# Two heads scored a batch ahead, their V beside the dense chain, in a two-layer decode kernel

## The chip, the core and the metric

The kernel runs on one core of one Trainium2 chip. The metric is the device time of one execution in microseconds; the median of several runs counts. A core has five engines with instruction queues of their own: TensorE (PE; its weight loads are PEld), VectorE (DVE), ScalarE (ACT), GpSimd (POOL) and SyncE (SP), which here only issues DMAs. TensorE writes to PSUM; the rest of the data lies in SBUF.

## The reference

Eight batches, one token each, pass twice through the same two blocks: attention over a cache, then a small MLP.

```python
def _A_ref(x, k_cache, v_cache, wq, wo):           # x: 8 x 1 x 448
    q = (x @ wq).reshape(8, 1, 16, 256).transpose(0, 2, 1, 3)
    k = jnp.repeat(k_cache, 2, axis=1)             # caches: 8 x 8 heads x 4096 x 256, bf16
    v = jnp.repeat(v_cache, 2, axis=1)
    p = _softmax(jnp.einsum("bhqd,bhkd->bhqk", q, k) * 256 ** -0.5)
    o = jnp.einsum("bhqk,bhkd->bhqd", p, v)
    return o.transpose(0, 2, 1, 3).reshape(8, 1, 4096) @ wo

def _B_ref(x, w1, w2, w3, w4):
    ...            # S = 1: every shifted part of h is zero, so x1 = x
    return x1 + _gelu(_layernorm(x1) @ w3) @ w4

x = x + _A_ref(_layernorm(x), ...)
x = x + _B_ref(_layernorm(x), ...)
x = x + _A_ref(_layernorm(x), ...)                 # the same caches and weights again
x = x + _B_ref(_layernorm(x), ...)
```

The caches are 134 MB each and are needed in both layers; everything else is small.

## The kernel before

**Units, parts and steps.** A unit `(p, b, g)` is one KV head `g` (two query heads) of batch `b` in pass `p` (1 for the first attention, 2 for the second). Its 4096 keys are four parts of 1024 keys, 512 KB of K and 512 KB of V each. The list `units` is the order of work. The main loop walks it, unit `t`, quarter `q`, and calls the pair a step, numbered `4 * t + q`. In a step, `k_part` (L573) multiplies one part of K by the spread query: 16 matmuls into scores. `v_part` (L552) multiplies one part of V by the exponentials of an earlier unit: 16 matmuls into the sum of its head. Between them stands the scoring of the unit before: `max_reduce` (L588, DVE), `max_mms` (L596, PE), `exps` (L606 DVE and L609 ACT), `to_rows` (L622 and L632 PE, L636 ACT) and `sums` (L643 DVE, L644 POOL). V part `s` of unit `t` comes in step `4 * t + s + LAG`, LAG being 6; those of the last unit before a chain come earlier, so that steps 4 and 5 of a chain have none. This is the dictionary `plan`.

**Slots.** All K and V pass through 31 slots of SBUF (512 KB each). `loads` is the list of loads in the order of their use. `pump` issues the next one from SyncE (L462) whenever a slot is free beyond one in reserve. A K part lands raw, is transposed by two DVE instructions into a second slot (`transposes`, L486), which frees the first. The list `by` spreads these transposes evenly over the steps between the borders of the chains. A V part frees its slot when `v_part` is through.

**Kept heads.** Of the eight heads of a batch, the K of six (2 to 7) is kept in its slots after pass 1 and used again in pass 2; the K of the "loose" heads 0 and 1 is read twice. Two parts of the 24 kept ones are parked in PSUM and copied back by ACT (L458). Around a chain, then, 22 of 31 slots hold kept K.

**Order of a batch.** Pass 1 of the kept heads; then the dense chain; then, behind a border called the fence, pass 2 of the kept heads. The dense chain (`mid_steps`, one piece a step) is the output projection (L175), layer norm (L204 to L239), the MLP (L131, L306), layer norm and the second q (L131, L338), all for one batch. Beside it stand units that need nothing of it: loose heads of pass 2 of earlier batches and of pass 1 of later ones.

```python
for b in range(Bn):
    units += [(1, b, g) for g in heads[(len(loose) if b else 0) :]]
    ends[len(units) - 1] = b
    n2 = (0, 2, 2, 2, 2, 2, 1, 3)[b]
    n1 = (4, 2, 2, 2, 1, 1, 2, 0)[b]
    units += [after.pop(0) for _ in range(n2)] + [early.pop(0) for _ in range(n1)]
    fence[len(units)] = b
    units += [(2, b, g) for g in second]
```

So four units (16 steps) stand beside each of the first four chains, three (12 steps) beside the others. `make_blocks` spreads q for a run of up to three heads (`expand`, L154 on PE, L160 on ACT), two steps before the run begins, or, at the fence, as soon as the new q is there. The last units are the two loose heads of pass 2 of the last batch; then comes the last MLP for all batches at once.

Of the kernel before, what the change touches and what calls it, by code (L numbers as in the profile page):

```python
# [17 lines left out]
RESERVE = 1  # L18
KEEP = 6
PARKED = 2  # L20
RUN = 3
LEAD = 1
LAG = 6

# [2 lines left out]
def kernel(  # L27
# [59 lines left out]


    qT1 = consts.tile([128, HJ, Bn], BF16, name="qT1")
    qT2 = consts.tile([128, HJ, 3], BF16, name="qT2")  # L90
    Qblk = [consts.tile([128, RUN, 4, 2, 4, 2], BF16, name=f"Qblk{i}") for i in range(2)]


# [73 lines left out]
    PO = 8 * Bn  # L167
    n_po = (512 - PO) // 4
    OT = consts.tile([128, HJ, 2], BF16, name="OT")

    def wo_mms(y, o, g):

# [81 lines left out]
    def mid_steps(b, spread):  # L254

        xs = X[:, b, :]
        res = {}

        def first():
            nc.vector.tensor_tensor(out=xs, in0=xs, in1=y1[:, b, :], op=ALU.add)
            total(xs)

        between.append(first)
        yield
        norm_rows(xs, res)
# [30 lines left out]

        between.append(gelu)
        yield  # L300
        yield
        yp = room(4)
        for cs in bursts(4, 2, spread):
            for c in cs:
                for m in range(HC):
                    nc.tensor.matmul(  # L306
                        yp[:, c : c + 1],
                        chunk(w4_sb[:, m, :], c),
                        hT[:, m : m + 1],
                        start=(m == 0),  # L310
                        stop=(m == HC - 1),
                    )
# [12 lines left out]
        yield  # L325

        variance(((256.0, 256.0 * EPS),))
        q2 = qT2[:, :, b % 3].rearrange("p (i m) -> p i m", i=2)
        qp = room(HJ).rearrange("p (i m) -> p i m", i=2)
        for ms in bursts(HJ // 2, 3 if spread else 2, True):  # L330
            in_mms(
                qp[:, :, ms[0] : ms[-1] + 1].unsqueeze(3), wq_sb, wq_tl, res["rows"], HJ, ms, True
            )
            if ms[-1] + 1 < HJ // 2:
                yield

        def scaled():
            nc.scalar.mul(q2, qp, nr[:, 0:1])  # L338
            q_done.add(b)

        between.append(scaled)
# [5 lines left out]

    second = heads[G - KEEP // 2 :] + heads[G - KEEP : G - KEEP // 2]
    parked = {(second[-1], 4 - PARKED + i): i for i in range(PARKED)}
    early = [(1, b, g) for b in range(1, Bn) for g in loose]  # L350
    after = [(2, b, g) for b in range(Bn - 1) for g in loose]
    units = []
    ends = {}
    fence = {}
    for b in range(Bn):
        units += [(1, b, g) for g in heads[(len(loose) if b else 0) :]]
        ends[len(units) - 1] = b

        n2 = (0, 2, 2, 2, 2, 2, 1, 3)[b]
        n1 = (4, 2, 2, 2, 1, 1, 2, 0)[b]  # L360
        units += [after.pop(0) for _ in range(n2)] + [early.pop(0) for _ in range(n1)]
        fence[len(units)] = b
        units += [(2, b, g) for g in second]
    units += [(2, Bn - 1, g) for g in loose]
    n_units = len(units)
    assert not early and not after and len(set(units)) == n_units == 2 * Bn * G

    def fresh(u, s):

        return u[0] == 1 or u[2] in loose  # L370


    runs = {}
    run_of = []
    t = 0
    while t < n_units:
        p, b, g = units[t]
# [29 lines left out]


    plan = {}
    for t in range(n_units):  # L410
        for s in range(4):
            i = 4 * t + s + LAG
            if t in ends:
                i = 4 * t + (6, 6, 7, 7)[s]
            elif t + 1 == n_units:
                i = 4 * t + (5, 5, 6, 7)[s]
            plan.setdefault(i, []).append((t, s))
# [4 lines left out]
    for i in range(4 * n_units + 8):  # L422
        while k < by[min(i, 4 * n_units - 1)]:
            loads.append(("k",) + parts[k])
            k += 1
        loads += [("v",) + p for p in plan.get(i, [])]
        t, q = divmod(i + 2, 4)
        if t < n_units and units[t][0] == 2 and (units[t][2], q) in parked:
            loads.append(("p", t, q))
    loads.reverse()  # L430
    free = list(slots)
# [61 lines left out]
            pump()  # L493


    pts, scs, mzs, pos = {}, {}, {}, {}
    dense = []

    def dense_next():
# [6 lines left out]
    def make_blocks(t):  # L506

        if t in runs and t not in ready:
            p, b, g = units[t]
            if p == 1 or b in q_done:  # L510
                x, n = runs[t]
                qT = qT1[:, :, b] if p == 1 else qT2[:, :, b % 3]
                expand(Qblk[x], qT[:, 4 * g : 4 * (g + n)], n, scb[t % 2])
                ready.add(t)

    def head_out(t):

        p, b, g = units[t]
        for h in range(2):
            k = 4 * g + 2 * h  # L520
            o = OT[:, k : k + 2, b % 2] if p == 1 else qT1[:, k : k + 2, b]
            nc.scalar.mul(o, pos[t][:, :, h], rzs[t % 2][:, h : h + 1])  # L522

    def mark(t):


        p, b, g = units[t]
        if p == 1:

            gs = [g]  # L530
            if b and g in loose:
                return
            if b and g - len(loose) in loose:
                gs = [g - len(loose), g]
            for k in gs:
                wo_mms(y1[:, b, :].unsqueeze(2), OT[:, :, b % 2 : b % 2 + 1], k)
        elif b == Bn - 1:
            wo_mms(y2, qT1, g)
        if t in ends:
            dense.append(mid_steps(b, spread[b]))  # L540

    def v_part(t, s):
        if s == 0:
            at = PO + 4 * (t % n_po)
            pos[t] = pyb[:, at : at + 4].rearrange("p (k h) -> p k h", h=2)
            if t == n_po // 2:
                nc.vector.memset(pyb[:, PO : PO + 4 * (n_units - n_po)], 0.0)
        v = v_of.pop((t, s))
        vv = v[:].rearrange("p (c d) -> p c d", d=Dh)
        for c in range(8):  # L550
# [66 lines left out]
    def to_rows(t):  # L617
# [12 lines left out]
        for c in range(4):  # L630
            sel = rows32[:, c].rearrange("p b r -> p (b r)")
            nc.tensor.matmul(pp[:, c], sel, pe[:], start=True, stop=True)  # L632
        pts[t] = work.tile([128, 32, 2], BF16, tag="pt", name="pt")
        for pb in range(4):
            sl = slice(32 * pb, 32 * pb + 32)
            nc.scalar.copy(  # L636
# [4 lines left out]
    def sums(t):  # L641
        zz = mzs[t][:, 256:320].rearrange("p (c h) -> p h c", h=2)
        nc.vector.tensor_reduce(zs, zz, AX.X, ALU.add)  # L643
        nc.gpsimd.tensor_tensor(out=rzs[t % 2], in0=zs, in1=mone, op=ALU.pow)  # L644


    identb = slots[-4][:, 1024:1152]
# [57 lines left out]
    for t in range(n_units + 1):  # L705
        cur = t < n_units
        for q in range(4):
            i = 4 * t + q
            if cur:
# [8 lines left out]
                flush()  # L718
                if not late and not beside[t]:
                    transposes(i)  # L720
                k_part(t, q)
            if q == 0 and t:
                max_mms(t - 1)
                exps(t - 1)
            if cur and late:
                transposes(i)
            if t and q == 1:
                to_rows(t - 1)
                sums(t - 1)
            if q == 2 and not cur:  # L730
# [9 lines left out]
            dense_next()  # L740
            if q > 1:
                make_blocks(t + 1)
            if cur and q == 3:
                max_reduce(t)
    mark(last)
    flush()
# [110 lines left out]
```

## Time and profile before

| | |
|---|---|
| median of 3 runs | 1132.48 us (1129.94 to 1134.14) |
| profiled execution: its own time, its span | 1134.93 us, 1133.2 us |
| read from HBM | 446.77 MB, 394 GB/s over the span |
| PE, DVE, ACT, POOL busy | 61%, 49%, 26%, 9% of the span |
| loads of V and K | 512 and 320, of 512 KB each |
| granted clock of TensorE | 1.000 |

The profile is of one execution. Its page has the busy shares, the span in 40 slices, the DMA queues, the chain of work that ended last, and the costliest groups of instructions. The trace behind it answers for stretches of time, lists who waited for whom, and shows instructions in the order of time, each with the idle time before it and what ended that in brackets. A name such as `SPq L462` is an engine (`q`: its queue) and a line of the kernel before.

### The profile page before, as it was taken

Reading aid. Unit: us, or ns where it says so; the run is one execution under the profiler, and the core shown is the slowest. Engines: PE = TensorE matmul, PEld = TensorE weight load, DVE = VectorE, ACT = ScalarE, POOL = GpSimd, SP = SyncE. Lnnn points to the kernel's source line nnn. Section 1 sums busy time; section 2 is a strip of 40 time slices with the busy share of each in tenths; the row PEclk is TensorE's granted clock in tenths of the full one; section 3 lists DMA queues with packets and bytes.
Section 4 is the critical chain, followed back from the end, with each engine's and each line's share of the span. In section 5 each row is a group of like instructions: output and inputs, shape, how many; then the busy total and the mean of one; then the engine's idle time right before and its main releaser. Section 6 shows DMA issues by size and latency. Waiting matters only on the chain.

```text
span 1133.2 us, 46689 instructions
## 1 busy us (share of the span) xinstructions
PE 689.6 (61%) x20665; PEld 624.5 (55%) x20665; DVE 556.7 (49%) x1305; ACT 293.1 (26%) x1280; POOL 104.2 (9%) x156
## 2 busy tenths in 40 slices
PE   3155665657656576565656666565765666565665
PEld 3144655556555565565655565565655565565665
DVE  5265645446454554545545464545544454546332
ACT  1012123222322223221232214222232214221241
POOL 0000010001000010000000010000100000000011
DMA  9999999999999999999999999999999999999993
GB/s 362 383 418 417 407 399 416 417 405 387 417 417 416 398 392 415 416 417 374 402 417 416 417 375 387 417 417 415 358 416 416 416 384 409 417 416 406 355 417 132
DMA packets 127194, 449.80 MB, mean 397 GB/s; under 512 B 13568, under 2 KB 19600, under 8 KB 126608
## 3 DMA queue, kind: packets, MB, share of 16 engines
q1 hardware_dynamic: 126992, 446.83, 98.9%
q8 instruction: 161, 2.64, 0.8%
q14 instruction: 41, 0.34, 0.1%
HBM read 446.77 MB, written 0.01 MB: 394 GB/s over the span
## 4 chain that ended last, share of the span: by engine, by line
DMA 71%; PE 13%; DVE 5%; issue 5%; ACT 3%; SPq 2%; POOL 0%; POOLq 0%; DVEq 0%; ACTq 0%
DMA slot<-in_A_v_cache_dram 42%; DMA slot<-in_A_k_cache_dram 28%; PE bank L552 3%; DVE slot L486 3%; PE bank L573 3%; PE bank L131 2%; SPq L462 2%; ACT pt L636 2%; PE bank L231 1%; PE bank L632 1%; ACT pe L609 1%; DVE small L606 1%; PE bank L596 0%; PE bank L622 0%; PE bank L139 0%
## 5 line engine op out<-in xcount | busy, mean ns | idle before, releaser
L552 PE MATMUL bank<-pt,slot 128*128 128x2 bf16 x8192 | 302.0, 166 | 361.3 <-DMA slot<-in_A_v_cache_dram 327.3
L552 PEld LDWEIGHTS <-slot 128*128 128x128 bf16 x8192 | 265.6, 105 | 414.7 <-DMA slot<-in_A_v_cache_dram 380.4
L486 DVE STREAM_TRANSPOSE slot<-slot 128x512 f32<-128x512 f32 x640 | 415.9, 688 | 146.7 <-DMA slot<-in_A_k_cache_dram 131.6
L573 PE MATMUL bank<-Qblk,slot 128*128 128x8 bf16 x8192 | 294.9, 168 | 24.2 <-issue 15.4
L573 PEld LDWEIGHTS <-slot 128*128 128x128 bf16 x8192 | 263.7, 104 | 28.7 <-issue 22.5
L644 POOL TENSOR_TENSOR small<-small 128x2 f32<-128x2 f32 x128 | 89.3, 698 | 970.7 <-DVE small L643 970.7
L609 ACT ACTIVATE pe<-bank,small 128x32 bf16<-128x32 f32 x256 | 61.1, 296 | 449.9 <-DVE small L606 449.9
L636 ACT CAST pt<-bank 32x64 bf16<-32x64 f32 x512 | 103.8, 203 | 142.8 <-PE bank L632 138.4
L606 DVE TENSOR_REDUCE small<-bank 128x2 f32<-128x256 f32 x128 | 54.0, 422 | 154.0 <-PE bank L596 154.0
L643 DVE TENSOR_REDUCE small<-bank 128x2 f32<-128x64 f32 x128 | 28.4, 221 | 160.9 <-ACT pt L636 119.6
L588 DVE TENSOR_REDUCE small<-bank 128x2 bf16<-128x64 f32 x128 | 27.2, 213 | 88.1 <-PE bank L573 88.0
L160 ACT CAST Qblk<-bank 32x48 bf16<-32x48 f32 (+2 forms) x200 | 37.4, 187 | 101.1 <-PE bank L154 87.3
L632 PE MATMUL bank<-pe,rows 128*128 128x64 bf16 x512 | 51.0, 241 | 0.0
L596 PE MATMUL bank<-rows,small 128*128 128x128 bf16 x256 | 48.0, 291 | 1.9 <-DVE small L588 1.9
L522 ACT ACTIVATE OT<-bank,small 128x2 bf16<-128x2 f32 x128 | 26.9, 261 | 70.1 <-PE bank L552 68.9
L175 PEld LDWEIGHTS <-wo_sb 128*128 128x128 bf16 x1152 | 35.4, 104 | 6.8 <-issue 6.8
L632 PEld LDWEIGHTS <-rows 128*128 128x128 bf16 x512 | 33.7, 124 | 8.6 <-issue 7.5
L175 PE MATMUL bank<-OT,wo_sb 128*128 128x1 bf16 x1024 | 33.1, 165 | 5.0 <-ACT OT L522 5.0
L131 PEld LDWEIGHTS <-wq_sb 128*128 128x128 bf16 x864 | 29.9, 106 | 8.5 <-DMA wq_sb<-in_A_wq_dram 4.5
L622 PE MATMUL bank<-pe,small 128*128 128x64 bf16 x128 | 27.3, 213 | 7.2 <-ACT pe L609 4.4
L458 ACT COPY slot<-park 128x1024 bf16<-128x1024 bf16 x32 | 30.8, 1015 | 3.1 <-PE bank L552 2.9
L522 ACT ACTIVATE qT<-bank,small 128x2 bf16<-128x2 f32 x128 | 27.0, 265 | 7.8 <-PE bank L552 4.2
(108 smaller groups left out, 321.3 us busy)
## 6 DMA issues: line engine op xcount, KB each, us to landing
slot<-in_A_v_cache_dram SPq DMA_DIRECT2D x512, 512.0 KB, 9.9
slot<-in_A_k_cache_dram SPq DMA_DIRECT2D x320, 512.0 KB, 9.9
wo_sb<-in_A_wo_dram SPq DMA_DIRECT2D x4, 896.0 KB, 9.3
wq_sb<-in_A_wq_dram SPq DMA_DIRECT2D x3, 1024.0 KB, 6.9
w_sb<-in_B_w_dram SPq DMA_DIRECT2D x1, 1568.0 KB
w_sb<-in_B_w_dram SPq DMA_DIRECT2D x3, 448.0 KB, 10.3
wq_tl<-in_A_wq_dram SPq DMA_DIRECT2D x2, 256.0 KB, 10.1
w_tl<-in_B_w_dram SPq DMA_DIRECT2D x2, 112.0 KB, 9.3
```

Of the source, the lines that this page charges most:

```text
L131: nc.tensor.matmul(pv[:, i, j, :], cols(big[:, c, :], m + i * half), rows[:, c, :], start=(i == 0 and j == 0 and c == 0), stop=True, skip_ ...
L175: nc.tensor.matmul(y[:, c, :], chunk(wo_sb[:, k, :], c), o[:, k, :], start=False, stop=True, skip_group_check=True,)
L486: nc.vector.transpose(dst[:, q], src[:, q])
L522: nc.scalar.mul(o, pos[t][:, :, h], rzs[t % 2][:, h : h + 1])
L552: nc.tensor.matmul(pos[t][:, k, :], vv[:, c, 128 * k : 128 * k + 128], pts[t][:, 8 * s + c, :], start=(t == 0 and s == 0 and c == 0 and k ...
L573: nc.tensor.matmul(scs[t][:, 2 * s + c, :, :], ktv[:, db, c, :, x], Qblk[run_of[t][0]][:, run_of[t][1], db, x, :, :], start=(db == 0 and x ...
L596: nc.tensor.matmul(mzs[t][:, 128 * h : 128 * h + 128], pm[:, h : h + 1].to_broadcast([128, 128]), ident, start=True, stop=True,)
L606: nc.vector.tensor_reduce(nm, mx, AX.X, ALU.max, negate=True)
L609: nc.scalar.activation(pe[:].rearrange("p c b h -> p h (c b)")[:, h], scs[t].rearrange("p c b h -> p h (c b)")[:, h], ACT.Exp, bias=nm[:, ...
L632: nc.tensor.matmul(pp[:, c], sel, pe[:], start=True, stop=True)
L636: nc.scalar.copy(pts[t][sl].rearrange("p (k c) h -> p k c h", c=4), pp[sl, :, :, pb, :].rearrange("p c k h -> p k c h"),)
L644: nc.gpsimd.tensor_tensor(out=rzs[t % 2], in0=zs, in1=mone, op=ALU.pow)
```

## The change

Every chain gets two units without K, `GAP`, one ahead of and one behind its one or two whole units (`lone`). In their four steps nothing is transposed for them or scored; V parts and the dense chain go on. Two heads a chain (`ahead`) are scored earlier: most of them are the loose heads of pass 2 of the batch before, which now stand in the middle of that batch's kept heads (third to fifth place behind the fence), and before the first chain two loose heads of pass 1 of batch 1. Their exponentials and reciprocals stay in tiles of their own (`pt_far`, `rz_far`), and their eight V parts are read and multiplied in steps 0, 1 and 4 to 9 of the next chain (`late_v`). The V parts of a whole unit that stands ahead of a `GAP` are due before the fence. The chains keep their 16 and 12 steps. `RUN` goes from 3 to 2, and the second q has two buffers instead of three. In all there are 144 units in place of 128, 16 of them `GAP`.

```diff
-RUN = 3
+RUN = 2
+AHEAD = 2
...
-    early = [(1, b, g) for b in range(1, Bn) for g in loose]
-    after = [(2, b, g) for b in range(Bn - 1) for g in loose]
+    GAP = None
+    ahead = {b: [(2, b - 1, g) for g in loose] for b in range(1, Bn)}
+    ahead[0], ahead[6] = [(1, 1, g) for g in loose], [(2, 5, 0), (1, 7, 0)]
+    lone = {b: [(1, b + 2, g) for g in loose] for b in range(4)}
+    lone.update({4: [(1, 6, 0)], 5: [(1, 6, 1)], 6: [(1, 7, 1)], 7: [(2, 5, 1)]})
...
+    late_v = {}
+    half = KEEP // 2
     for b in range(Bn):
-        units += [(1, b, g) for g in heads[(len(loose) if b else 0) :]]
+        if b:
+            units += [(1, b, g) for g in heads[len(loose) :]]
+        else:
+            units += [(1, b, g) for g in heads[:-half]] + ahead[0] + [(1, b, g) for g in heads[-half:]]
         ends[len(units) - 1] = b
-
-        n2 = (0, 2, 2, 2, 2, 2, 1, 3)[b]
-        n1 = (4, 2, 2, 2, 1, 1, 2, 0)[b]
-        units += [after.pop(0) for _ in range(n2)] + [early.pop(0) for _ in range(n1)]
+        at = 4 * len(units)
+        ps = [(units.index(u), s) for u in ahead[b] for s in range(4)]
+        late_v.update(zip(ps, [at + i for i in (0, 1, 4, 5, 6, 7, 8, 9)]))
+        units += [GAP] + lone[b] + [GAP]
         fence[len(units)] = b
-        units += [(2, b, g) for g in second]
+        units += [(2, b, g) for g in second[:half]] + ahead.get(b + 1, []) + [(2, b, g) for g in second[half:]]
     units += [(2, Bn - 1, g) for g in loose]
...
-    for t in range(n_units):
+    for t in order:
         for s in range(4):
-            i = 4 * t + s + LAG
-            if t in ends:
+            i = late_v.get((t, s), 4 * t + s + LAG)
+            if t in ends or units[t + 1 : t + 2] == [GAP]:
                 i = 4 * t + (6, 6, 7, 7)[s]
...
-        pts[t] = work.tile([128, 32, 2], BF16, tag="pt", name="pt")
+        if (t, 0) in late_v:
+            held.append(t)
+            pts[t] = work.tile([128, 32, 2], BF16, tag="pt_far", name="pt_far", bufs=AHEAD)
+        else:
+            pts[t] = work.tile([128, 32, 2], BF16, tag="pt", name="pt")
...
-        nc.gpsimd.tensor_tensor(out=rzs[t % 2], in0=zs, in1=mone, op=ALU.pow)
+        rz_of[t] = rzs[nth[t] % 2]
+        if (t, 0) in late_v:
+            rz_of[t] = rz_far[:, held.index(t) % AHEAD, :]
+        nc.gpsimd.tensor_tensor(out=rz_of[t], in0=zs, in1=mone, op=ALU.pow)
...
-                k_part(t, q)
-            if q == 0 and t:
+                if units[t]:
+                    k_part(t, q)
+            back = t and units[t - 1]
+            if q == 0 and back:
                 max_mms(t - 1)
                 exps(t - 1)
```

More of the change, by code (lines that the diff above doesn't have):

```diff
@@ L89 @@
     qT1 = consts.tile([128, HJ, Bn], BF16, name="qT1")
-    qT2 = consts.tile([128, HJ, 3], BF16, name="qT2")
+    qT2 = consts.tile([128, HJ, 2], BF16, name="qT2")
     Qblk = [consts.tile([128, RUN, 4, 2, 4, 2], BF16, name=f"Qblk{i}") for i in range(2)]
@@ L169 @@
     OT = consts.tile([128, HJ, 2], BF16, name="OT")
+    rz_far = consts.tile([128, AHEAD, 2], FP32, name="rz_far")
     def wo_mms(y, o, g):
@@ L327, in mid_steps @@
         variance(((256.0, 256.0 * EPS),))
-        q2 = qT2[:, :, b % 3].rearrange("p (i m) -> p i m", i=2)
+        q2 = qT2[:, :, b % 2].rearrange("p (i m) -> p i m", i=2)
         qp = room(HJ).rearrange("p (i m) -> p i m", i=2)
@@ L354 @@
     fence = {}
+    late_v = {}
+    half = KEEP // 2
     for b in range(Bn):
-        units += [(1, b, g) for g in heads[(len(loose) if b else 0) :]]
+        if b:
+            units += [(1, b, g) for g in heads[len(loose) :]]
+        else:
+            units += [(1, b, g) for g in heads[:-half]] + ahead[0] + [(1, b, g) for g in heads[-half:]]
         ends[len(units) - 1] = b
-        n2 = (0, 2, 2, 2, 2, 2, 1, 3)[b]
-        n1 = (4, 2, 2, 2, 1, 1, 2, 0)[b]
-        units += [after.pop(0) for _ in range(n2)] + [early.pop(0) for _ in range(n1)]
+        at = 4 * len(units)
+        ps = [(units.index(u), s) for u in ahead[b] for s in range(4)]
+        late_v.update(zip(ps, [at + i for i in (0, 1, 4, 5, 6, 7, 8, 9)]))
+        units += [GAP] + lone[b] + [GAP]
         fence[len(units)] = b
-        units += [(2, b, g) for g in second]
+        units += [(2, b, g) for g in second[:half]] + ahead.get(b + 1, []) + [(2, b, g) for g in second[half:]]
     units += [(2, Bn - 1, g) for g in loose]
     n_units = len(units)
-    assert not early and not after and len(set(units)) == n_units == 2 * Bn * G
+    order = [t for t in range(n_units) if units[t]]
+    nth = {t: n for n, t in enumerate(order)}
+    assert len({units[t] for t in order}) == len(order) == 2 * Bn * G
     def fresh(u, s):
-        return u[0] == 1 or u[2] in loose
+        return u is not GAP and (u[0] == 1 or u[2] in loose)
     runs = {}
@@ L376 @@
     while t < n_units:
+        if units[t] is GAP:
+            run_of.append(None)
+            t += 1
+            continue
         p, b, g = units[t]
@@ L427 @@
         t, q = divmod(i + 2, 4)
-        if t < n_units and units[t][0] == 2 and (units[t][2], q) in parked:
+        if t < n_units and units[t] and units[t][0] == 2 and (units[t][2], q) in parked:
             loads.append(("p", t, q))
@@ L493, in transposes @@
             pump()
-    pts, scs, mzs, pos = {}, {}, {}, {}
+    pts, scs, mzs, pos, rz_of, held = {}, {}, {}, {}, {}, []
     dense = []
@@ L511, in make_blocks @@
                 x, n = runs[t]
-                qT = qT1[:, :, b] if p == 1 else qT2[:, :, b % 3]
+                qT = qT1[:, :, b] if p == 1 else qT2[:, :, b % 2]
                 expand(Qblk[x], qT[:, 4 * g : 4 * (g + n)], n, scb[t % 2])
@@ L521, in head_out @@
             o = OT[:, k : k + 2, b % 2] if p == 1 else qT1[:, k : k + 2, b]
-            nc.scalar.mul(o, pos[t][:, :, h], rzs[t % 2][:, h : h + 1])
+            nc.scalar.mul(o, pos[t][:, :, h], rz_of[t][:, h : h + 1])
     def mark(t):
+        if units[t] is GAP:
+            return
         p, b, g = units[t]
@@ L543, in v_part @@
         if s == 0:
-            at = PO + 4 * (t % n_po)
+            at = PO + 4 * (nth[t] % n_po)
             pos[t] = pyb[:, at : at + 4].rearrange("p (k h) -> p k h", h=2)
-            if t == n_po // 2:
-                nc.vector.memset(pyb[:, PO : PO + 4 * (n_units - n_po)], 0.0)
+            if nth[t] == n_po // 2:
+                nc.vector.memset(pyb[:, PO : PO + 4 * (len(order) - n_po)], 0.0)
         v = v_of.pop((t, s))
@@ L726 @@
                 transposes(i)
-            if t and q == 1:
+            if back and q == 1:
                 to_rows(t - 1)
@@ L742 @@
                 make_blocks(t + 1)
-            if cur and q == 3:
+            if cur and units[t] and q == 3:
                 max_reduce(t)
```

## The prediction

> **What bounds the kernel now.** I read the page first: busy shares, the chain that ended last, the DMA lines.
>
> ```profile
> DMA  9999999999999999999999999999999999999993
> GB/s 362 383 418 417 407 399 416 417 405 387 417 417 416 398 392 415 416 417 374 402 417 416 417 375 387 417 417 415 358 416 416 416 384 409 417 416 406 355 417 132
> DMA 71%; PE 13%; DVE 5%; issue 5%; ACT 3%; SPq 2%; POOL 0%; POOLq 0%; DVEq 0%; ACTq 0%
> ```
>
> The DMA share hides the dips; the rate below it shows them. Most slices run at 416 to 418 GB/s; about eight times the rate sinks to 358 to 400. The chain is 71% DMA, and nearly every byte is cache that must be read (832 loads of 512 KB), so time can only come out of the dips, the start or the tail. The change leaves start and tail alone.
>
> Next, busy time by stretch. The rows of the first block are stretches around a dense chain (last head of pass 1, chain, first units of pass 2); the row of the second is a stretch between chains. Columns: window, length, busy of PE, PEld, DVE, ACT, POOL, clock, DMA share, GB/s.
>
> ```profile
> 98.00:165.00 67.00, 41.76 (x1239) 38.09 (x1236) 37.18 (x91) 14.60 (x70) 6.13 (x9) 1.00 1.02 405
> 504.00:570.00 66.00, 42.55 (x1266) 39.02 (x1263) 36.03 (x90) 14.70 (x70) 6.13 (x9) 1.00 1.00 392
> 640.00:696.00 56.00, 36.26 (x1104) 33.83 (x1100) 30.09 (x78) 12.91 (x62) 5.43 (x8) 1.00 0.99 381
> 765.00:823.00 58.00, 37.12 (x1118) 34.45 (x1116) 30.00 (x78) 12.90 (x62) 5.43 (x8) 1.00 1.00 387
> 1016.00:1072.00 56.00, 36.73 (x1111) 34.12 (x1108) 28.44 (x75) 12.91 (x62) 5.43 (x8) 1.00 0.99 381
> ```
> ```profile
> 696.00:765.00 69.00, 43.20 (x1307) 38.40 (x1304) 32.79 (x67) 21.32 (x88) 6.28 (x9) 1.00 1.03 416
> ```
>
> Loss of a stretch = length × (417 − rate) / 417. With the three rows not shown (399, 397 and 396 GB/s in 66, 66 and 54 us) that is 1.9, 2.8, 3.2 and 4.0 us for the four chains of 16 steps and 4.8, 4.2, 2.7 and 4.8 for the four of 12 steps: 11.9 + 16.5 = **28.4 us**, all that can be won.
>
> Third, the sixth chain close up: SyncE's issues, then TensorE.
>
> ```profile
> 805.64 0.80 SPq L462 DMA_DIRECT2D slot<-in_A_v_cache_dram  x2
> 812.35 0.33 SPq L462 DMA_DIRECT2D slot<-in_A_k_cache_dram  x1
> ```
> ```profile
> 805.90 0.23 PE L154 MATMUL bank<-qT,rows 128*128 128x12 bf16 x3
> 808.78 0.17 PE L154 MATMUL bank<-qT,rows 128*128 128x12 bf16 x1 [2.65 <-issue]
> 809.84 0.57 PE L573 MATMUL bank<-Qblk,slot 128*128 128x8 bf16 x16 [0.89 <-ACT Qblk L160]
> ```
>
> At the fence no load is issued for over 6 us. The kept K tiles hold their slots until the new q is spread, and V parts already landed hold theirs until their step comes (LAG is 6). By the issue and landing times, loads outstanding fall from 6 to 2; those issued at 812.77 and 813.98 then land 2.56 and 2.41 us after the one before, instead of 1.25. A shallow queue costs bandwidth.
>
> Fourth, who waits inside the chains: the third (16 steps), then the sixth (12 steps).
>
> ```profile
> PE bank L552 <- DMA slot<-in_A_v_cache_dram: 4.9, 3, 2.7
> DVE slot L486 <- DMA slot<-in_A_k_cache_dram: 5.5, 5, 1.9
> ```
> ```profile
> PE bank L154 <- issue: 2.7, 1, 2.7
> PE bank L231 <- DVE small L222: 1.4, 2, 0.9
> ```
>
> The long chains still wait for data now and then. The short ones do not: TensorE is late there, and landed data sits in slots.
>
> **The change, part by part.** *Loads.* None is removed: 512 V and 320 K before and after, 16 parked copies in both. Only order and lifetime change.
>
> *The chain's steps.* Counted from the plan, a long chain before has 16 K parts transposed and scored and 16 V parts multiplied; after, 8 and 22. A short chain has 12 and 12, then 4 and 18. A part is 16 matmuls, 0.43 us on TensorE either way (the starts at 802.70 and 803.12). Scoring a unit (L596, L622, L632) is 0.37 + 0.21 + 0.40 = 0.98 us; two units fewer are scored in either chain and just behind its fence. So TensorE saves 2 × 0.43 + 2 × 0.98 = 2.8 us of a chain. VectorE loses eight parts of two 0.69 us transposes (1.3 us a part, L486) and two units of 0.42 + 0.22 + 0.21: 12 us of a chain. That work stood ahead of the chain's small operations on the same engine (center, scale, gelu).
>
> *Slots.* From step 4 of a short chain to its fence, slots given back are 8 K + 6 V before and 4 K + 10 V after: 14 both times. Steps 4 and 5, which before have no V part at all, have one each. The larger difference is at the fence: before, the last unit's six remaining V parts straddle it; after, the K-less unit has multiplied every V part due, and the eight slots that hold raw K or V belong to loads for later steps. I expect 5 to 7 outstanding where the trace shows 4 to 6, some 9 us of transfers at 1.25 us each, which covers the 4 us of 805.9 to 809.8.
>
> *What it gives back.* Behind the fence the first six steps now have no V part, so one slot comes free a step and not two; another eight V-less steps follow at the two heads scored ahead. A step of a kept unit with its V part takes 1.1 to 1.5 us there once data has landed (TensorE's K parts start at 813.96, 815.21, 816.27 and 817.78), without V some 0.4 less: about one slot a microsecond, against one load per 1.25 us. Balanced, with the queue as reserve. Bounds: nothing, or 0.5 us for each of 14 steps in eight batches, 56 us, if a V-less step lasted 1.75 us. The rows lie near the first end; I put 2 us.
>
> *Smaller parts.* RUN 2 makes 76 spreads of q instead of 50: 26 × 4 casts of 187 ns (L160) = 19 us more on ScalarE, which is 26% busy, and 26 × 0.25 us on TensorE. Each is made two steps ahead, behind L636 and L522 of the unit before; who waits is the next K part, which in the whole trace waited 4.6 us for it in five places. Between chains TensorE is busy 43 of 69 us, so this hides under loads; without that cover it is up to 26 us. Held exponentials and reciprocals go to tiles of their own, the same casts and the same 0.70 us GpSimd power: nothing. No queue is passed by anything new: SyncE issues in the new order, and the parked copies (L458, 1.0 us each) stay behind the same units. The V wait in front of the chain's first addition comes behind two more V loads, 2.5 us, within a stretch that its loads fill anyway: nothing. The two K-only heads before the first chain cost VectorE 1.5 us a step (1.3 + a quarter of 0.85) against 1.25 us of load for eight steps, 2 us, under 19 loads of reserve: nothing.
>
> **The sum.** In the long chains TensorE and VectorE work shrinks while loads still set the pace: I take three quarters of 11.9 us, 9. In the short ones as many slots come free for as much TensorE time, so mainly the hole at the fence closes: a quarter of 16.5, 4. Less 2 behind the fences: 11 us. The profiled execution took 1134.93 us (span 1133.2 and 1.7 around it), which gives 1124; it stands 2.4 us over the median, 1132.48, which gives **1121.5**.
>
> On the shallow queue: with three and four loads outstanding the trace has 2.4 us and more between landings. The Trainium skill ("DMA: Bandwidth & Descriptors", Anatomy of one DMA) puts a fixed 2 us plus bytes at 436 GB/s on a DMA, fitted on another issuing path; by that, as an estimate, a load alone takes 3.2 us and three outstanding keep the rate. The trace disagrees with it.
>
> **Rivals.** *Every hole closes.* If the queue never runs shallow the whole 28.4 us come back: 1104. For it: the eight slots at the fence. Against it: nearly as many slots come free for nearly as much TensorE time in a short chain. (The page's fixed cost would give the same, since five outstanding would then be more than enough.)
>
> *Same holes, other place.* The 14 = 14 slots above speak for it: short chains keep their 16.5, the long ones win some 4 and the fences take 2 back: gain 0 to 5, 1127.5 to 1133. Against it: six V parts stuck at the fence are gone.
>
> *Slower: V-less steps starve the queue.* One slot a step in the 14 V-less steps of a batch. It decides once such a step lasts over 1.25 us by more than the queue covers; at 1.75 us a batch loses 14 × 0.5 = 7 us, some 5 beyond the cover, 40 in eight batches, less the 11 won: 1161. For it: scoring is a round trip over four engines (L588, L596, L606, L609, L632), with no V work between. Against it: those kept units with V run at 1.1 to 1.5 us a step.
>
> *Slower: TensorE's clock.* K-less units leave TensorE waiting for V loads. If the granted clock halved there, 28 parts and some 8 us of chain matmuls would take up to 20 us longer in a chain, half of it beyond the loads: some 80 us, 1200. Against it: in the slice from 40 to 50 us TensorE was busy 1.0 of 10 us and the granted clock stayed 1.00. The Trainium skill ("TensorE: Matmul & The Clock Gate", What's actually happening) says that the clock halves after about 3.4 us idle; that slice speaks against it.
>
> **How the numbers follow.** A measurement of this kernel can tell about 0.5% (5.7 us) from no change. The forecast (gain 6 to 20) has 0.56, every hole closed 0.04, same holes 0.21, V-less starvation 0.16, the clock 0.03: faster 0.60, same 0.21, slower 0.19. The low end of the range is a gain of 20 (1112), the high end takes in the same holes and a mild starvation (1138). The forecast's own range is 1112 to 1127.
>
> **What would show it.** Right: the chain stretches at 400 GB/s or more, no issue hole over 4 us at a fence, outstanding loads never under 3, K parts behind the fence about 1 us apart, the stretches between at 416, clock 1.00. Wrong: dips just behind the fences or at the two heads scored ahead, TensorE waiting there for scores, or short chains still at 381 to 387.

## The result and the profile after

| | before | after |
|---|---|---|
| median of 20 runs each, us | 1133.53 (1129.94 to 1135.78) | 1136.01 (1133.76 to 1139.9) |
| ratio after / before | | 1.0025, 95% interval 1.0015 to 1.0035 |
| profiled execution: own time, span, us | 1134.93, 1133.2 | 1135.04, 1133.0 |

The changed kernel is slower by 0.25%. That is inside the half per cent that the prediction called "same", but the interval excludes no change. The forecast was a gain of 11 us. The two profiled executions differ by 0.1 us only: that of before lies above its median, that of after below its own. So the traces show where time moved, and the 2.5 us between the medians have to come from the timed runs.

The page of after: the rate in the 40 slices, the chain of work that ended last by engine, and the spreads of q (group row; busy and mean ns, then idle before).

```profile
GB/s 361 386 417 418 413 391 415 417 416 399 416 416 417 407 392 413 417 417 400 406 415 417 417 396 358 417 416 417 363 400 417 416 411 372 416 417 417 372 415 77
DMA 66%; PE 16%; DVE 6%; issue 5%; ACT 4%; SPq 2%; POOL 0%; POOLq 0%; DVEq 0%; ACTq 0%
L161 ACT CAST Qblk<-bank 32x32 bf16<-32x32 f32 (+1 forms) x304 | 53.0, 174 | 81.8 <-PE bank L155 78.0
```

The dips of the first four chains are shallower in sum, those of the last four are still there (358, 363, 372, 372). The chain of waits has moved five points away from DMA: three to TensorE, one each to VectorE and ScalarE. The casts of q cost 15.6 us more on ScalarE (37.4 us before).

Busy time by stretch in after: one long chain and the four short ones, a stretch between chains, then the end of the kernel in two parts. Columns: window, length, busy of PE, PEld, DVE, ACT, POOL, clock, DMA share, GB/s.

```profile
109.00:168.00 59.00, 37.17 (x1096) 34.00 (x1092) 27.53 (x72) 11.91 (x58) 4.75 (x7) 1.00 1.02 403
646.00:706.00 60.00, 39.80 (x1187) 36.78 (x1185) 25.22 (x68) 13.77 (x68) 4.75 (x7) 1.00 0.98 379
772.00:832.00 60.00, 39.68 (x1198) 36.93 (x1194) 25.20 (x68) 13.70 (x68) 4.75 (x7) 1.00 0.98 384
899.00:955.00 56.00, 36.93 (x1121) 34.52 (x1119) 23.59 (x65) 12.52 (x62) 4.75 (x7) 1.00 0.99 391
1024.00:1080.00 56.00, 35.93 (x1080) 33.51 (x1078) 19.73 (x59) 14.14 (x63) 4.75 (x7) 1.00 1.00 393
706.00:772.00 66.00, 41.17 (x1232) 37.74 (x1230) 37.34 (x77) 22.18 (x95) 6.99 (x10) 1.00 1.03 416
1080.00:1112.00 32.00, 22.27 (x713) 21.32 (x711) 9.23 (x23) 11.98 (x52) 2.86 (x5) 1.00 0.96 388
1112.00:1133.00 21.00, 11.17 (x327) 10.53 (x327) 5.26 (x25) 2.74 (x12) 4.64 (x5) 1.00 0.01 3
```

By the prediction's formula the long chains lose 7.9 us instead of 11.9 (rates 403, 408, 399 and 402 in 59, 63, 58 and 56 us), the short ones 16.9 instead of 16.5. VectorE is relieved in the short chains (25 of 60 us, 30 of 56 to 58 before); TensorE is not (39.8 of 60, 36.3 of 56 before). Between chains the rate is 416 as before, and the clock is 1.00 everywhere.

The last row is the other half of the story. Before, it reads:

```profile
1116.00:1133.20 17.20, 7.95 (x221) 7.29 (x220) 4.62 (x23) 2.18 (x10) 4.01 (x4) 1.00 0.01 3
```

In after the last load landed at 1111.5 us, 4.5 us earlier than before (1116.1). But the work behind it took 21.5 us instead of 17.1. The stream won 4.5 us and the tail gave back 4.4.

**The sixth chain in after**, as shown of before: SyncE's issues (start, duration to the last of the group, count), TensorE, VectorE, then TensorE's waits from 783 to 822 us (total, times, longest).

```profile
807.96 0.33 SPq L478 DMA_DIRECT2D slot<-in_A_k_cache_dram  x1
808.39 0.38 SPq L478 DMA_DIRECT2D slot<-in_A_v_cache_dram  x1
812.83 0.33 SPq L478 DMA_DIRECT2D slot<-in_A_k_cache_dram  x1
813.26 4.49 SPq L478 DMA_DIRECT2D slot<-in_A_v_cache_dram  x2
```
```profile
811.95 0.21 PE L132 MATMUL bank<-small,wq_sb 128*128 128x1 bf16 x2 [2.37 <-issue]
812.24 0.99 PE L569 MATMUL bank<-pt,slot 128*128 128x2 bf16 x32
813.09 0.25 PE L155 MATMUL bank<-qT,rows 128*128 128x8 bf16 x4
814.35 2.28 PE L590 MATMUL bank<-Qblk,slot 128*128 128x8 bf16 x80 [1.01 <-ACT Qblk L161]
818.74 0.40 PE L613 MATMUL bank<-rows,small 128*128 128x128 bf16 x2 [2.11 <-DVE small L605]
```
```profile
814.75 3.83 DVE L502 STREAM_TRANSPOSE slot<-slot 128x512 f32<-128x512 f32 x6 [7.05 <-PE bank L590]
818.50 0.18 DVE L605 TENSOR_REDUCE small<-bank 128x2 bf16<-128x64 f32 x1
```
```profile
PE bank L569 <- DMA slot<-in_A_v_cache_dram: 5.0, 6, 1.9
PE bank L132 <- issue: 2.4, 1, 2.4
PE bank L613 <- DVE small L605: 2.1, 1, 2.1
PE bank L590 <- ACT Qblk L161: 1.0, 1, 1.0
```

TensorE's waits for loads (L569, 5.0 us) all lie before 792 us, ahead of the dense chain. Later its data has long landed: the V parts of the chain's last two steps, the last two of them at 812.24, were through 4.4 to 7.6 us after landing. Until then SyncE has no free slot: from 808.39 to 812.83 it issues nothing. Behind the new q five K parts run off in 2.28 us (L590 x80), faster than any load. VectorE had nothing to do for 7.05 us before that, and now stands with three parts to transpose (3.83 us) in front of the `max_reduce` (L605) that TensorE waits for. Loads outstanding fall to 2 at 816.6. Before had one stretch of 6.3 us without an issue here (806.07 to 812.35); after has two, 4.4 us ahead of the spread of the new q and 4.2 us behind it (813.26 to 817.42). At the four short fences the fewest outstanding is 2, 2, 2 and 3; around the same fences in before it is 3.

**The end of the kernel.** The last rows of TensorE with cache in them, before, then after.

```profile
1118.74 0.99 PE L552 MATMUL bank<-pt,slot 128*128 128x2 bf16 x32
1120.31 0.56 PE L175 MATMUL bank<-qT,wo_sb 128*128 128x8 bf16 x16 [0.57 <-ACT qT L522]
```
```profile
1118.62 0.99 PE L569 MATMUL bank<-pt,slot 128*128 128x2 bf16 x32
1120.18 0.57 PE L177 MATMUL bank<-qT,wo_sb 128*128 128x8 bf16 x16 [0.57 <-ACT qT L538]
```

The same work at the same time, within 0.13 us. Before, the last V part had landed 2.7 us before its group starts; in after the last landing was 7.1 us before it. The data came earlier, its use did not. Behind the last q TensorE has no listed wait for a load in before, and one of 0.6 us in after.

### The profile page after: what moved, and what is told of

It reads as the page before. It is cut to its first block, busy times and chain, and to the rows that moved or that the text cites. A ratio compares the mean times of both kernels' runs of the same rounds, so it can differ in the third digit from the quotient of the medians.

```text
span 1133.0 us, 47063 instructions
## 1 busy us (share of the span) xinstructions
PE 700.0 (62%) x20769; PEld 641.9 (57%) x20769; DVE 554.9 (49%) x1305; ACT 308.1 (27%) x1384; POOL 104.4 (9%) x156
## 4 chain that ended last, share of the span: by engine, by line
DMA 66%; PE 16%; DVE 6%; issue 5%; ACT 4%; SPq 2%; POOL 0%; POOLq 0%; DVEq 0%; ACTq 0%
DMA slot<-in_A_v_cache_dram 43%; DMA slot<-in_A_k_cache_dram 22%; PE bank L569 5%; DVE slot L502 4%; PE bank L590 3%; PE bank L132 2%; SPq L478 2%; ACT pt L657 1%; PE bank L613 1%; PE bank L177 1%; DVE small L623 1%; ACT pe L626 1%; PE bank L308 1%; PE bank L649 1%; ACT slot L474 1%
## 5 line engine op out<-in xcount | busy, mean ns | idle before, releaser
L569 PEld LDWEIGHTS <-slot 128*128 128x128 bf16 x8192 | 268.9, 105 | 335.0 <-DMA slot<-in_A_v_cache_dram 300.8
L569 PE MATMUL bank<-pt,slot 128*128 128x2 bf16 x7168 | 260.8, 166 | 269.0 <-DMA slot<-in_A_v_cache_dram 237.4
L590 PE MATMUL bank<-Qblk,slot 128*128 128x8 bf16 x8192 | 294.4, 168 | 41.6 <-issue 19.5
L590 PEld LDWEIGHTS <-slot 128*128 128x128 bf16 x8192 | 266.6, 105 | 49.0 <-issue 33.2
L668 POOL TENSOR_TENSOR small<-small 128x2 f32<-128x2 f32 x112 | 78.4, 700 | 779.6 <-DVE small L664 779.6
L657 ACT CAST pt<-bank 32x64 bf16<-32x64 f32 x448 | 91.1, 203 | 108.1 <-PE bank L649 103.7
L161 ACT CAST Qblk<-bank 32x32 bf16<-32x32 f32 (+1 forms) x304 | 53.0, 174 | 81.8 <-PE bank L155 78.0
L613 PE MATMUL bank<-rows,small 128*128 128x128 bf16 x256 | 48.6, 293 | 18.9 <-DVE small L605 18.8
L569 PE MATMUL bank<-pt_far,slot 128*128 128x2 bf16 x1024 | 37.6, 166 | 25.1 <-DMA slot<-in_A_v_cache_dram 22.6
L605 DVE TENSOR_REDUCE small<-bank 128x2 bf16<-128x64 f32 x128 | 25.5, 199 | 35.4 <-PE bank L590 35.0
```

Of the source, the lines that this page charges most:

```text
L161: nc.scalar.copy(dst, src)
L569: nc.tensor.matmul(pos[t][:, k, :], vv[:, c, 128 * k : 128 * k + 128], pts[t][:, 8 * s + c, :], start=(t == 0 and s == 0 and c == 0 and k ...
L590: nc.tensor.matmul(scs[t][:, 2 * s + c, :, :], ktv[:, db, c, :, x], Qblk[run_of[t][0]][:, run_of[t][1], db, x, :, :], start=(db == 0 and x ...
L613: nc.tensor.matmul(mzs[t][:, 128 * h : 128 * h + 128], pm[:, h : h + 1].to_broadcast([128, 128]), ident, start=True, stop=True,)
L657: nc.scalar.copy(pts[t][sl].rearrange("p (k c) h -> p k c h", c=4), pp[sl, :, :, pb, :].rearrange("p c k h -> p k c h"),)
L668: nc.gpsimd.tensor_tensor(out=rz_of[t], in0=zs, in1=mone, op=ALU.pow)
```

## The experiments

Each ratio is against the kernel before, measured beside the run on the same chip. Two times are used from the traces: "last q", the end of the scaling of the last chain's q (L338; L340 in after), and "last landing". Behind the last q every kernel has the same eight heads of pass 2 to score, 32 K parts. Single profiles of one kernel differ by some 2 us (`long_only` and `long_only2` are the same kernel), so the ratios decide, and the marks only say where. Nor is the last column the form's doing alone: behind the last q TensorE stands with no releaser in the trace ("issue") for 8.5 us in before, 10.9 to 12.6 us in the kernels with `RUN = 2`, the old last chain and nothing thinned, and 8.0 to 10.2 us in those with the new last chain.

| kernel | ratio (95% interval) | last q | last landing | end less last q |
|---|---|---|---|---|
| before | 1 | 1059.9 | 1116.1 | 73.3 |
| after | 1.0025 (1.0015 to 1.0035) | 1061.6 | 1111.5 | 71.4 |
| `run2` | 0.9984 (0.9969 to 0.9999) | 1055.7 | 1113.5 | 77.0 |
| `last_old` | 0.9993 (0.9977 to 1.0009) | 1056.0 | 1111.8 | 75.0 |
| `long_only` | 0.9975 (0.9959 to 0.9991) | 1052.7 | 1111.7 | 76.2 |
| `long_only2` | 0.9981 (0.9964 to 0.9997) | 1055.0 | 1112.6 | 76.1 |
| `short_only` | 1.0016 (1.0000 to 1.0032) | 1062.1 | 1112.3 | 70.8 |
| `hoist` | 1.0006 (0.9995 to 1.0018) | 1063.2 | 1113.2 | 71.7 |
| `hoist_last_old` | 0.9995 (0.9978 to 1.0011) | 1055.2 | 1110.5 | 75.3 |
| `long_hoist` | 1.0005 (0.9992 to 1.0017) | 1054.7 | 1112.4 | 75.5 |
| `lag` | 1.0034 (1.0022 to 1.0046) | 1063.4 | 1113.4 | 71.0 |
| `thin_short` | 0.9961 (0.9946 to 0.9977) | 1054.0 | 1103.5 | 71.0 |
| `tail_before` | 0.9965 (0.9946 to 0.9984) | 1059.9 | 1115.8 | 69.6 |
| `tail_after` | 0.9991 (0.9979 to 1.0004) | 1062.6 | 1113.2 | 66.4 |

**`run2`: the small part alone.** The kernel before with one constant changed.

```diff
-RUN = 3
+RUN = 2
```

> The kernel before with RUN = 2 alone. Theory of the tail (the change won about 4.5 us in the stream of loads, and lost them again because TensorE reaches the last fence 4.4 us later and sets the pace behind it): nothing, 1133.5 within 1.5. Rival, the smaller runs: 26 more spreads of q cost ScalarE and TensorE time on the path, and RUN 2 by itself is the 2 to 3 us of the changed kernel: 1136. A third view, that both weigh: 1134.5 to 1135.

Measured: 1132.63 us, 0.9984. The further casts are hidden, as the prediction had it. That the kernel came out slightly faster was not expected, and its cause is not settled (the interval ends at 0.9999). Its last load landed some 2.5 us earlier than in before.

**`last_old`, `long_only`, `short_only`: the change by chains.** The changed kernel, but the chains in `OLD` are made as before: `(7,)`, `(4, 5, 6, 7)` and `(0, 1, 2, 3)`. Heads scored ahead for such a chain stand beside it again.

```diff
-        at = 4 * len(units)
+        if b in OLD:
+            units += ahead[b] + lone[b]
+        else:
+            at = 4 * len(units)
...
-            ... + ahead.get(b + 1, []) + ...
+            ... + ([] if b + 1 in OLD else ahead.get(b + 1, [])) + ...
```

> The changed kernel, but the last chain as before: three whole units beside it, no K-less unit, no head scored ahead for it. Theory of the tail: six V parts go back behind the last fence, the fence comes about 4 us earlier, and the 4 us won in the stream reach the end: 1131 to 1132. Rival, the smaller runs: 1135 to 1136. Rival, the holes of all four short chains count alike: a quarter of what they lose, about 1135.

> The changed kernel with K-less units and heads scored ahead for the first four (16-step) chains alone; the four 12-step chains as before. Theory of the tail, with the windows (long chains lose 7.9 instead of 11.9 us, short ones 16.9 instead of 16.5): the 4 us stay won and the end is as before: 1129 to 1130, the last landing about 4 us earlier than before and the tail behind it about 17 us. Rival, the smaller runs: 1132 to 1134. If the holes merely move to the next short chain: 1133.

> The reverse: only the four 12-step chains are changed, the 16-step ones as before. Theory of the tail: nothing won in the stream, the last fence later: 1136 to 1138, with new holes of the load queue just behind the fences. Rival, the smaller runs: 1135 to 1136, the same for long and short chains alone.

Measured: 0.9993, 0.9975 and 1.0016. Giving only the last chain back its old form takes 1.0025 to 0.9993, about 3.6 us: the last q comes at 1056.0 instead of 1061.6, and the end follows, though the last landing hardly moves (1111.8 and 1111.5). Giving the other short chains back as well adds 1.4 to 2 us (`long_only2`, `long_only`), but these intervals overlap with that of `last_old`. The short chains' form costs: `short_only` has it alone, at 1.0016 (from 1.0000), and against `run2`, which it contains, that is 3.6 us. The long chains' form does not cost. But `long_only` cannot be told from `run2`, which it contains too.

The rate over the stretch from 60 to 600 us, which holds the four long chains, says how little is left for their form. The rows are before, `run2`, after and `hoist` (below).

```profile
60.00:600.00 540.00, 333.40 (x9949) 299.70 (x9946) 282.59 (x637) 141.30 (x620) 48.93 (x71) 1.00 1.02 408
60.00:600.00 540.00, 336.32 (x10045) 302.72 (x10045) 284.29 (x640) 149.83 (x672) 49.05 (x71) 1.00 1.02 410
60.00:600.00 540.00, 340.66 (x10038) 310.50 (x10036) 285.23 (x645) 150.41 (x678) 49.76 (x72) 1.00 1.02 411
60.00:600.00 540.00, 339.65 (x9948) 308.37 (x9946) 283.36 (x641) 148.99 (x670) 49.05 (x71) 1.00 1.02 407
```

By the formula that is 11.7, 9.1, 7.8 and 12.9 us lost. With the old form of the long chains two more executions read 411 (`short_only`, with `RUN = 2`) and 409 (`tail_before`, with `RUN = 3`). So of the 4 us between before and after about 1 is left for the new form, no more than executions differ by.

**`hoist`: the transposes behind the fence made earlier.** If the new hole comes from three transposes standing in front of `max_reduce`, the four parts can be transposed during the `GAP` ahead of the fence, when VectorE is idle.

```diff
         by[i] = max(by[i], sum(4 * p[0] + p[1] <= i + LEAD for p in parts))
+    for f in fence:
+        if units[f - 1] is GAP:
+            for j in range(4):
+                by[4 * f - 4 + j] = max(by[4 * f - 4 + j], by[4 * f - 5] + j + 1)
+    for i in range(1, 4 * n_units):
+        by[i] = max(by[i], by[i - 1])
```

> The changed kernel with four K transposes, one a step, in the K-less unit behind each chain, so that none is due in the first steps behind the fence. Theory of the burst: in the changed kernel three transposes (3.8 us, 814.75 to 818.58) stand ahead of the first max_reduce behind the fence while five K parts are through in 2.3 us; TensorE waits 2.1 us for it, and the queue of loads runs dry because its slots hang on that. Taking the burst away wins 1 to 2 us at each short chain and 2 at the last fence: 1130 to 1133. Rival, TensorE late from the chain's own matmuls and its issue stalls: 1136, unchanged, the holes behind the short chains as large.

TensorE and VectorE at the same place in `hoist` (line numbers are six higher):

```profile
816.81 2.28 PE L596 MATMUL bank<-Qblk,slot 128*128 128x8 bf16 x80 [1.02 <-ACT Qblk L161]
819.05 0.40 PE L619 MATMUL bank<-rows,small 128*128 128x128 bf16 x2
```
```profile
818.77 0.23 DVE L611 TENSOR_REDUCE small<-bank 128x2 bf16<-128x64 f32 x1 [5.11 <-PE bank L596]
```

The 2.11 us wait of TensorE (L613 in after) is gone: the reduction follows the K parts directly. The fewest loads outstanding at the short fences are now 4, 3, 3 and 3, and the short chains' windows of after read 397, 392, 391 and 388 GB/s, 13.9 us lost instead of 16.9. The ratio falls to 1.0006, some 2 us. So the wait and its share of the short chains' hole are shown. The time, 1133.78 us, misses the range of 1130 to 1133, the intervals of `hoist` and after overlap (0.9995 to 1.0018, 1.0015 to 1.0035), and the last landing of this execution, 1113.2, is not earlier. The long chains say why: from 60 to 600 us the rate falls from 411 in after to 407, 5 us more lost by the formula, and the fewest loads outstanding at each of their four fences fall from 4 or 5 to 3. What the transposes win at the short fences they lose at the long ones.

**`lag`: the V parts of the unit ahead of a `GAP` due as late as other units' are.**

```diff
-            if t in ends or units[t + 1 : t + 2] == [GAP]:
+            if t in ends:
```

> The changed kernel, but V parts of a whole unit ahead of a K-less one at the usual LAG of 6, not all before the fence: in the long chains two parts move behind the fence, in the short ones none but spread over four steps instead of two. Theory of the tail and of the slots: nothing to within 2 us, 1134 to 1137. Rival, that the crowd of V parts in the last two steps makes TensorE late at the fence: 1 us a chain, 1128 to 1131.

Measured: 1.0034, no better than the change (1.0025) and, if anything, worse. That V parts were pulled ahead of the fence by this rule is not what costs.

**`tail_before`, `tail_after`: less TensorE work behind the last q.** In the V parts of the last four units only 2 of 16 matmuls are made, in the kernel before and in the changed one. All loads stay. That takes 16 x 14/16 x 0.43 = 6 us off TensorE.

```diff
-        for c in range(8):
+        for c in range(1 if t >= n_units - 4 else 8):
```

> The kernel before with 2 instead of 16 matmuls in each V part of the last four units (sums cut as in tail_after). If there the loads set the end, as in the trace (last landing 1116.1, then 17.1 us): 1 to 2 us won, 1131.5 to 1133. If TensorE set it there too: 3 to 6 us, 1127 to 1130, and then the change did not move the bound.

> The changed kernel with 2 instead of 16 matmuls in each V part of the last four units (the sums of these heads leave out most of the cache; the loads are all there): 6 us less TensorE work behind the last fence. Theory of the tail, TensorE and the scoring set the end: 3 to 6 us earlier, 1130 to 1133. Rival, the last loads set the end: within 1 us of 1136.

The time from the last q to the end falls from 73.3 to 69.6 us in the kernel before and from 71.4 to 66.4 in the changed one; the ratios fall from 1 to 0.9965 and from 1.0025 to 0.9991. By the ratios that is 4.0 and 3.9 us. Both kernels end mainly at TensorE's pace, not only the changed one; that the kernel before would do so too I had not expected. The last landing did not move with it in `tail_before` (1115.8 against 1116.1). The change did not move the bound at the end; the prediction had never seen it.

**`thin_short`: less TensorE work in three short chains.** The changed kernel with 2 of 16 matmuls in the V parts of nine units, three beside each of chains 5 to 7. All loads stay. That is 12 parts x 14/16 x 0.43 = 4.5 us less TensorE work a chain.

```diff
-        for c in range(8):
+        thin = units[t] in [u for c in (4, 5, 6) for u in ahead[c] + lone[c]]
+        for c in range(1 if thin else 8):
```

> The changed kernel with 2 instead of 16 matmuls in the V parts of the nine units beside chains 5 to 7 (their sums leave out most of the cache; every load is there): 4.5 us less TensorE work in each of these chains, the last chain whole. Theory that TensorE's lateness makes the holes of the short chains: these three lose 2 to 4 us less each, the last landing is 6 to 10 us earlier than in the changed kernel, and the end follows, because the last chain still waits for loads: 1127 to 1131. Rival, the slots alone make the holes: 1134 to 1137.

Busy time of `thin_short` in the stretches of the four short chains; the last of them is not thinned.

```profile
646.00:706.00 60.00, 36.70 (x1046) 33.14 (x1043) 27.43 (x73) 14.34 (x70) 5.44 (x8) 1.00 1.02 407
772.00:832.00 60.00, 36.46 (x1048) 32.98 (x1046) 27.03 (x72) 15.96 (x74) 5.43 (x8) 1.00 1.02 404
899.00:955.00 56.00, 34.78 (x984) 31.34 (x982) 25.19 (x68) 14.77 (x67) 4.74 (x7) 1.00 1.02 406
1024.00:1080.00 56.00, 36.45 (x1119) 34.56 (x1117) 17.35 (x56) 16.16 (x66) 4.74 (x7) 1.00 0.98 379
```

The three thinned chains rise from 379, 384 and 391 to 407, 404 and 406 GB/s. The last landing comes 8.0 us earlier than in after, the last q 7.6 us, and the ratio falls from 1.0025 to 0.9961, 7.3 us. With the same slots, loads and order, less TensorE work alone takes what these three chains lose, by the formula, from 13.7 to 4.8 us: TensorE holds them up, not the number of slots given back. It was not tried on the kernel before. From the last q to the end it is 71.0 us, as in after (71.4): the end keeps its distance from the last q.

**`hoist_last_old`, `long_hoist`, `long_only2`: the repairs together.** The transposes of `hoist` in `last_old` and in `long_only`, and `long_only` once more beside them.

> The changed kernel with both repairs: four K transposes drawn into the K-less unit behind each of the first seven chains, and the last chain as before. If the two add up (2 us for the transposes, 3.6 for the last chain): 1129 to 1131, ratio 0.997. If the transposes only helped behind the last fence: 1131 to 1133, ratio 0.999.

> K-less units at the four 16-step chains alone (1130.85 in the first runs), and four transposes drawn into the K-less unit behind each. Theory of the burst: up to 1 us a chain, 1127 to 1130. Rival: in long chains TensorE still waits for loads, so the burst is hidden: 1130 to 1132.

> K-less units at the 16-step chains alone, once more, beside the others on one chip. Theory of the tail: 4 us won in the stream and kept, ratio 0.9965. What the first runs leave open: 0.9975 here and 1.0005 with the transposes drawn ahead; if the first was partly luck, 0.999.

Measured: 0.9995, 1.0005 and 0.9981. The repairs do not add up: with the old last chain, `hoist` brings nothing beyond 0.9993, and in the long chains alone it costs (1.0005 against 0.9975 and 0.9981). The rates show the two halves. From 60 to 600 us (long chains) the three kernels with `hoist` read 407, 407 and 408 GB/s, after, `last_old` and `long_only` 411; from 600 to 982 us (chains 5 to 7) `hoist` and `hoist_last_old` read 406 and 408, after and `last_old` 402 and 401. In `long_hoist` as in `hoist` 3 loads are outstanding behind each long fence. That the transposed parts, loaded earlier, hold slots over the fence there is my reading of the order of loads; it was not tried by itself. `long_only`, run twice, has the lowest times of those that compute everything, 1130.85 and 1131.53 us, below both kernels but not told apart from `run2`.

## Why the prediction was wrong

**The step that failed: "time can only come out of the dips, the start or the tail. The change leaves start and tail alone."** The sum let the end follow the load stream one to one. The stream did end 4.5 us earlier, and the tail behind it grew by 4.4 us, since the stretch behind the last q is set mainly by TensorE: of 6 us of its work taken away there, 3.7 (`tail_before`) and 5.0 us (`tail_after`) came off in the traces, 4.0 and 3.9 by the ratios. What then counts is when the last q is there and how much TensorE work stands behind it. The new last chain has six V parts more in front of its q, with five more loads landed by then (794 against 789). Kernels with that form and nothing thinned have the last q at 1061.6 to 1063.4 and the end 70.8 to 71.7 later; those with `RUN = 2` and the old last chain have it at 1052.7 to 1056.0, and the end 75.0 to 77.0 later. So the new form of the last chain costs more ahead of the q than it saves behind it: 3.6 us by the ratios of after and `last_old` (with `hoist` in both only 1.2, and there the intervals overlap). 2 to 3 us of what it seems to save are fewer stalls with no releaser. That it is these six V parts (2.6 us of TensorE at 0.43 us each; their loads, at 1.25 us each, are 7.5 us of the stream) and nothing else of the new form was not tried by itself. The 71% of DMA in the chain of waits hid this: that is a share of the whole span, and says nothing about its last stage. The stream does count as far as the last q follows it: in `thin_short` the last landing came 8.0 us earlier, the last q 7.6 and the end 7.3. But the two terms of the sum that were to speed it up were mis-sized as well.

**The short chains: 4 us expected, -0.4 measured (16.5 to 16.9).** The counts of parts and slots were right (14 slots for 14) and the reading of before too: "TensorE is late there". But I let eight freed slots cover the hole, and slots come free only when TensorE gets to the V parts in them. It gets there 4 to 8 us after they land. The 2.8 us less of work in a chain was too much: scoring a unit was priced by durations that overlap, 0.98 us, where the starts in before (797.65 to 797.82, 799.26 to 799.50) give 0.41, so it is 1.7 us. Neither brings the slots free in time; `thin_short` took 4.5 us more out of a chain, and then most of the hole closed. (The fewest loads outstanding at the sixth fence in before are 3, not 2: the trace lacks one landing there, and at the regular spacing that load was still on its way.) Behind the fence the five K parts at once and the three transposes then make a new hole, of which the prediction had only the V-less steps; `hoist` takes 3.0 us off what the short chains lose in its trace (16.9 to 13.9); its 2 us by the ratios are within the intervals.

**The long chains: 9 us expected, 4.0 measured (11.9 to 7.9).** Three quarters were taken where a third came, and most of that third comes with `RUN = 2` alone, as the rows from 60 to 600 us show; what is left for the form, about 1 us, is not clear of noise. The fewest loads outstanding at their fences are 4 or 5, before and after.

**What held.** `RUN = 2` costs nothing. Loads are the same 512 + 320. The stretches between the chains, with the heads scored ahead in them, stay at 416 GB/s, so the rival of V-less steps starving the queue (1161 us) did not occur, and the clock stayed at 1.00, with matmuls still 27 ns apart behind 6.2 us of idle time (50.27 us in before), so that rival (1200) did not either. Holes stay in the chains, so nor did the one in which all close (1104). Nearest was *same holes, other place*: short chains keep their holes, and the stream wins some 4 us. Its 14 = 14 slots were the argument to follow; its time, 1127.5 to 1133, still let the end follow the loads and so came out 3 us too low at its slow end. 1 us of that is its base: before has a median of 1132.48 in the three runs used there and 1133.53 in the 20 here.

**What stays open**: why `RUN = 2` alone comes out 0.16% faster, whether the long chains' form wins anything beyond that, what in the last chain's form delays the last q, and where TensorE's stalls with no releaser come from.

## What to carry to other kernels

Before crediting a filled hole to the total, find what sets the pace of the last stage: with the new last chain the end stood 70.8 to 71.7 us behind the last q while the last landing lay anywhere from 1103.5 to 1113.4, so a change is to be counted by what it puts in front of that q. Freeing buffers helps only if the engine that empties them is in time; where landed data waits for TensorE, take work from TensorE or move it, and count what it does in a burst when a wait ends. A change made of several parts at places with different limits is worth trying part by part: here the form of the long chains did no harm and that of the short ones, where TensorE is the limit, did.

## What the runs showed of the hardware

TensorE stands still inside its dense bursts with no releaser in the trace ("issue"), ten times for 1.5 to 3.8 us in before and ten times for 1.5 to 2.4 us in after (2.37 us ahead of the last piece of the q projection at 811.95; 2.23 us at 1110.50 in before, shortly before the end).

With a full queue a load takes 9.9 us from issue to landing and the rate is 416 GB/s. With few loads outstanding the spacing grows: between 60 and 1085 us in after, a load issued with three others outstanding landed on average 1.88 us after the one before (six loads), with four others 1.46 us (17 loads), with five or more 1.28 to 1.29 us (landings that the trace lacks are put midway when counting). That is milder than the 2.4 us and more that the prediction read off two loads. By the fixed cost in the Trainium skill ("DMA: Bandwidth & Descriptors", Anatomy of one DMA), fitted there on another issuing path, a load alone takes 3.2 us and three outstanding would, as an estimate, keep the rate; the 1.88 us here with four disagree with it again.
